# One decode step of cached attention with a ReGLU block: a hand-written program in place of a scheduled one

## The chip, the cores and the metric

The kernel runs on one core of a Trainium2 chip. TensorE (PE) multiplies, VectorE (DVE), ScalarE (ACT) and GpSimd (POOL) work elementwise, SyncE (SP) issues loads; each runs its own instruction queue in order. Sixteen DMA engines carry every load from HBM to the core's memory (SBUF). The metric is the device time of one execution in microseconds.

## The reference

One token `x` (640 values) goes through a layer norm, attention over a cache of 8192 keys and values per head, and a gated block, each with its residual. All data is float32.

```python
H, Dh, Sk, D, F = 32, 192, 8192, 640, 1536
xn = layernorm(x)
q  = (xn @ wq)                               # (H, Dh)
s  = einsum("hd,hkd->hk", q, k_cache) * Dh**-0.5
o  = einsum("hk,hkd->hd", softmax(s), v_cache)
h  = x + o.reshape(H * Dh) @ wo
g  = layernorm(h)
gate = g @ W_gate; gate = gate * (gate > 0)
out = h + (gate * (g @ W_up)) @ W_down
```

K and V are 201 MB each, wq and wo 15.7 MB each, W_up, W_gate and W_down 3.9 MB each: 446 MB that are read once.

## The kernel before

The program is written against a tile framework: pools of buffers hand out tiles, and the framework adds the waits. The order on each engine is the order of the code.

A head's 8192 positions are cut into two tiles of 4096 (`load_kv`, L77). In a tile, partition p holds 32 neighbouring positions, so that each partition's row is one run of 32 x 192 x 4 = 24 KB and a tile is 3 MB. Six buffers of 24 KB rows (pool `kv`) serve K, V, at the start wq and at the end the weights of the gated block.

For a head, `query` (L165) copies the head's q to all partitions through TensorE into PSUM. `scores_of` (L171) multiplies K with q on VectorE, 16 positions an instruction (L178), sums 10 of the 16 on VectorE (L179) and 6 on ScalarE, an instruction each (L181). `softmax_of` (L185) takes the maximum over all partitions through TensorE (L189, L193), then the exponential on ScalarE with its sums (L198) and the total through TensorE (L200). `values_of` (L212) multiplies the weights with V on TensorE, two positions of each partition a matmul, in four groups of rows (L217); `to_columns` (L223) adds the groups through TensorE (L232) and transposes on VectorE (L235).

The loop over heads (L246) issues the loads of K of the next head and V of this one in turn, then the work on V of this head, then scores and softmax of the next. wo is loaded in nine pieces (`load_wo`, L85), each ahead of the first of its four heads (the last two pieces have two heads each), and multiplied behind the last of them (`output_of`, L237). The weights of the gated block are loaded last, in eleven pieces, each as its buffer comes free (L283 to L290). The second layer norm (L295 to L313), the products with W_up and W_gate (L319), the gate (L329) and the product with W_down (L337) follow.

SP issues all of these loads in the order of the code, and a load whose buffer is still in use holds up the loads behind it.

Of the kernel before, what the change touches and what calls it, by code (L numbers as in the profile page):

```python
# [1 line left out]

# [8 lines left out]
AX = mybir.AxisListType  # L11


@with_exitstack
def kernel(
    ctx: ExitStack,
    tc: tile.TileContext,
    x: bass.AP,
    kc: bass.AP,
    vc: bass.AP,  # L20
    wq: bass.AP,
    wo: bass.AP,
    w_gate: bass.AP,
    w_up: bass.AP,
    w_down: bass.AP,
    out: bass.AP,
):
    nc = tc.nc
# [4 lines left out]
    DJ = D // P  # L33
    R = 32
    NCH = S // (P * R)
    NS = S // P
    SUB = 16
    NA = 6
    TW = R * DH
    HPQ = H // NQ  # L40
    QB = 512
    NQB = HPQ * DH // QB
    DG = D // NQ
    FG = F // NQ
    FJ = F // P
    SCALE = DH ** -0.5
    EPS = 1e-5
    GROUPS = [list(range(4 * i, 4 * i + 4)) for i in range(7)] + [[28, 29], [30, 31]]
    group_of = {h: (gi, i) for gi, hs in enumerate(GROUPS) for i, h in enumerate(hs)}
# [3 lines left out]
    const = ctx.enter_context(tc.tile_pool(name="const", bufs=1))  # L53
    kv = ctx.enter_context(tc.tile_pool(name="kv", bufs=6))
    wts = ctx.enter_context(tc.tile_pool(name="wts", bufs=2))
    small = ctx.enter_context(tc.tile_pool(name="small", bufs=2))
    row = ctx.enter_context(tc.tile_pool(name="row", bufs=1))
    ps_q = ctx.enter_context(tc.tile_pool(name="ps_q", bufs=2, space=bass.MemoryType.PSUM))
    ps_x = ctx.enter_context(tc.tile_pool(name="ps_x", bufs=1, space=bass.MemoryType.PSUM))
    ps_o = ctx.enter_context(tc.tile_pool(name="ps_o", bufs=1, space=bass.MemoryType.PSUM))  # L60
    ps_s = ctx.enter_context(tc.tile_pool(name="ps_s", bufs=2, space=bass.MemoryType.PSUM))
    ps_a = ctx.enter_context(tc.tile_pool(name="ps_a", bufs=1, space=bass.MemoryType.PSUM))

    xT = const.tile([P, DJ], F32, name="xT")
    xrow = const.tile([1, D], F32, name="xrow")
    nc.scalar.dma_start(xT, x[0, 0].rearrange("(p j) -> p j", p=P))
    nc.scalar.dma_start(xrow, x[0])


    wq_v = wq.rearrange("(p j) n -> p j n", p=P)  # L70
    wq_ts = []
    for j in range(DJ):
        t = kv.tile([P, TW], F32, name="kv_t")
        nc.sync.dma_start(t, wq_v[:, j, :])
        wq_ts.append(t)

    def load_kv(src, h, c, parts=1):  # L77
        t = kv.tile([P, TW], F32, name="kv_t")
        v = src[h, c * P * R:(c + 1) * P * R, :].rearrange("(p r) d -> p (r d)", p=P)
        n = TW // parts  # L80
        for i in range(parts):
            nc.sync.dma_start(t[:, i * n:(i + 1) * n], v[:, i * n:(i + 1) * n])
        return t

    def load_wo(gi):  # L85
        hs = GROUPS[gi]
        j = len(hs) * DH // P
        t = wts.tile([P, j, D], F32, tag="wo_t", name="wo_t")
        r0 = hs[0] * DH
        nc.sync.dma_start(t, wo[r0:r0 + len(hs) * DH, :].rearrange("(p j) n -> p j n", p=P))  # L90
        return t

    ones = const.tile([P, P], F32, name="ones")
    nc.vector.memset(ones, 1.0)
    eps = const.tile([P, 1], F32, name="eps")
    nc.vector.memset(eps, EPS)
    ident = const.tile([P, P], F32, name="ident")
    from concourse.masks import make_identity
    make_identity(nc, ident)

    sel = const.tile([P, NQ, P], F32, name="sel")
    nc.gpsimd.memset(sel, 0.0)
# [105 lines left out]
    for po in pos:  # L208
        nc.vector.memset(po, 0.0)
# [159 lines left out]
```

## Time and profile before

| | before |
|---|---|
| time, median of 3 runs | 1054.98 us (1054.37 to 1055.05) |
| profiled execution, first to last instruction (span) | 1052.8 us |
| median of the runs over that span | 2.2 us |
| PE, DVE, ACT, POOL busy | 438.6, 727.2, 325.1, 1.9 us |
| bytes moved, mean rate over the span | 446.48 MB, 424 GB/s |
| DMA packets | 22662 |
| mean granted clock of TensorE | 0.668 |

The profiled execution has no time of its own beside its span; the span covers what its instructions show. Busy times are sums over an engine's instructions. The slices that the prediction shows cut the span into 40 equal parts: a DMA digit is the mean busy share of the 16 DMA engines in tenths, and the row below it what they moved. The queue lines give packets, MB and the share of 16 engines' time that the packets took; q1 is SP's queue, q8 and q14 carry instructions, q10 is ScalarE's queue. In a group's row stand line, engine, operation, out<-in, shape, count, then busy us and mean ns of one, then the idle time of the engine ahead of it and what ended it. In the timeline a row is start, us, engine and line, operation and count. Matrix products in float32 leave two records each.

### The profile page before, as it was taken

To read this page: it belongs to the slowest core of one execution; us is meant where nothing else is said; L and a number is where in the kernel's file an instruction comes from. 1 tells how busy PE (TensorE), PEld (TensorE's weight loads), DVE (VectorE), ACT (ScalarE), POOL (GpSimd) and SP (SyncE) were. 2 spreads that over 40 slices of the span, in tenths; PEclk is the share of its full clock that TensorE was granted. 3 is DMA by queue.
4 is the path that set the end of the run, shared out by engine and by line. 5 is a ranking of instruction groups with operands and counts; after the bars stand their busy time and mean duration, and the time that the engine had idled before them with its cause. 6 is when DMAs were issued, how large, how long until landed. Compare 5 with 4: busy or idle time off the path is not lost.

```text
span 1052.8 us, 8858 instructions
## 1 busy us (share of the span) xinstructions
PE 438.6 (42%) x3136; PEld 136.1 (13%) x3136; DVE 727.2 (69%) x418; ACT 325.1 (31%) x1676; POOL 1.9 (0%) x11
## 2 busy tenths in 40 slices
PE   3423444344444333433442444344335334432466
PEld 1101111111111010111110111111101111110122
DVE  1188877677867777687776778677876877777641
ACT  0143333223323332232232333233322322333230
POOL 0000000000000000000000000000000000000000
PEclk9756666666666666766666665766667666666667
DMA  9999999999999999999999999999999999999996
GB/s 394 429 429 431 431 427 430 429 431 431 430 430 427 431 430 428 432 429 429 432 430 430 429 430 430 427 431 430 430 425 433 431 430 430 429 430 429 428 421 247
DMA packets 22662, 446.48 MB, mean 424 GB/s; under 512 B 2645, under 2 KB 2649, under 8 KB 4442
## 3 DMA queue, kind: packets, MB, share of 16 engines
q1 hardware_dynamic: 22472, 445.92, 99.1%
q8 instruction: 24, 0.39, 0.2%
q14 instruction: 20, 0.16, 0.0%
q10 hardware_dynamic: 146, 0.01, 0.0%
HBM read 445.91 MB, written 0.00 MB: 424 GB/s over the span
## 4 chain that ended last, share of the span: by engine, by line
DMA 65%; DVE 25%; PE 8%; ACT 1%; issue 1%; SPq 0%
DMA kv_t<-in_A_k_cache_dram 53%; DVE kv_t L178 18%; DMA kv_t<-in_A_v_cache_dram 8%; DVE sc L179 6%; PE po L217 5%; DMA dn_a<-in_B_W_down_dram 2%; DMA kv_t<-in_A_wq_dram 2%; PE q L168 1%; PE ps_small L232 1%; ACT p L198 0%; PE qp L159 0%; PE ps_small L193 0%; PE ps_small L200 0%; DVE oT L235 0%; PE pd L337 0%
## 5 line engine op out<-in xcount | busy, mean ns | idle before, releaser
L178 DVE TENSOR_TENSOR kv_t<-kv_t,q 128x3072 f32<-128x3072 f32 x128 | 423.4, 3349 | 163.4 <-DMA kv_t<-in_A_k_cache_dram 163.0
L181 ACT ACTIVATE kv_t<-kv_t 128x192 f32<-128x192 f32 x768 | 267.6, 349 | 529.5 <-DVE kv_t L178 529.5
L217 PE MATMUL po<-kv_t,p 128*2 128x384 f32 x2048 | 296.0, 747 | 245.6 <-DMA kv_t<-in_A_v_cache_dram 245.6
L179 DVE TENSOR_REDUCE sc<-kv_t 128x10 f32<-128x1920 f32 x128 | 269.1, 2144 | 0.0
L168 PE MATMUL q<-q,sel 128*128 128x192 f32 x64 | 31.0, 589 | 290.4 <-DVE kv_t L178 290.4
L181 ACT ACTIVATION_READ_ACCUMULATOR kv_t<-kv_t 128x1 f32 x768 | 143.3, 187 | 0.0
L217 PEld LDWEIGHTS po<-kv_t,p 128*2 128x2 f32 x2048 | 60.3, 111 | 449.8 <-DMA kv_t<-in_A_v_cache_dram 271.4
L168 PEld LDWEIGHTS q<-q,sel 128*128 128x128 f32 x64 | 15.7, 303 | 319.4 <-DVE kv_t L178 243.0
L220 ACT ACTIVATE ob<-po,rl 128x384 f32<-128x384 f32 x32 | 18.6, 580 | 113.5 <-PE po L217 113.5
L202 DVE RECIPROCAL rl<-ps_small 128x1 f32<-128x1 f32 x32 | 5.4, 168 | 52.6 <-PE ps_small L200 52.6
L191 DVE TENSOR_REDUCE m<-ps_small 1x1 f32<-1x128 f32 x32 | 8.9, 279 | 42.3 <-PE ps_small L189 42.3
L235 DVE STREAM_TRANSPOSE oT<-ps_small 32x192 f32<-32x192 f32 (+1 forms) x32 | 11.8, 367 | 27.1 <-PE ps_small L232 27.1
L232 PE MATMUL ps_small<-ob,par 128*32 128x192 f32 (+1 forms) x144 | 25.7, 315 | 0.7 <-ACT ob L220 0.7
L159 PE MATMUL qp<-kv_t,xn 128*32 128x512 f32 x120 | 19.4, 801 | 10.1 <-DMA kv_t<-in_A_wq_dram 9.1
L200 PE MATMUL ps_small<-rs,ones 128*128 128x1 f32 x64 | 12.4, 264 | 24.9 <-ACT p L198 24.9
L241 PE MATMUL acc<-wo_t,oT 128*32 128x160 f32 (+1 forms) x408 | 19.9, 352 | 4.6 <-DVE oT L235 4.6
L193 PE MATMUL ps_small<-m,ones 1*128 1x1 f32 x64 | 12.3, 259 | 11.9 <-DVE m L191 11.9
L241 PEld LDWEIGHTS acc<-wo_t,oT 128*32 128x32 f32 (+1 forms) x408 | 14.0, 127 | 9.9 <-DVE oT L235 7.8
L200 PEld LDWEIGHTS ps_small<-rs,ones 128*128 128x128 f32 x64 | 9.7, 191 | 27.6 <-ACT p L198 27.6
L193 PEld LDWEIGHTS ps_small<-m,ones 1*128 1x128 f32 x64 | 9.6, 186 | 18.3 <-DVE m L191 18.3
L232 PEld LDWEIGHTS ps_small<-ob,par 128*32 128x32 f32 x144 | 11.3, 109 | 4.8 <-ACT ob L220 1.4
L198 ACT ACTIVATE p<-sc,nb 128x64 f32<-128x64 f32 x32 | 11.1, 348 | 1.2 <-ACT nb L195 0.2
(77 smaller groups left out, 79.9 us busy)
## 6 DMA issues: line engine op xcount, KB each, us to landing
kv_t<-in_A_k_cache_dram SPq DMA_DIRECT2D x64, 3072.0 KB, 33.7
kv_t<-in_A_v_cache_dram SPq DMA_DIRECT2D x63, 3072.0 KB, 39.7
kv_t<-in_A_wq_dram SPq DMA_DIRECT2D x5, 3072.0 KB, 20.7
wo_t<-in_A_wo_dram SPq DMA_DIRECT2D x7, 1920.0 KB, 43.0
kv_t<-in_A_v_cache_dram SPq DMA_DIRECT2D x4, 768.0 KB, 38.3
up_a<-in_B_W_up_dram SPq DMA_DIRECT2D x1, 3072.0 KB, 33.9
gt_a<-in_B_W_gate_dram SPq DMA_DIRECT2D x2, 1536.0 KB, 24.2
wo_t<-in_A_wo_dram SPq DMA_DIRECT2D x2, 960.0 KB, 41.4
```

Source lines behind the costliest of these rows:

```text
L159: nc.tensor.matmul(qps[b][g * Q:(g + 1) * Q, :], xn[:, j:j + 1].to_broadcast([P, Q]), wq_ts[j][:, c0:c0 + QB], start=(j == 0), stop=(j == ...
L168: nc.tensor.matmul(q[:, 0:DH], sel[:, g, :], q4[:, i * DH:(i + 1) * DH], start=True, stop=True)
L178: nc.vector.tensor_mul(ks, ks, q[:, None, :].to_broadcast([P, SUB, DH]))
L179: nc.vector.reduce_sum(sc[:, i0:i0 + SUB - NA], ks[:, :SUB - NA, :], axis=AX.X)
L181: nc.scalar.activation(ks[:, r, :], ks[:, r, :], AF.Copy, accum_out=sc[:, i0 + r:i0 + r + 1])
L193: nc.tensor.matmul(pb[:, 0:1], ones[0:1, :], m1, start=True, stop=True)
L200: nc.tensor.matmul(pl[:, 0:1], ones, rs, start=True, stop=True)
L217: nc.tensor.matmul(po[g * Q:g * Q + 2, :], p[:, 2 * i:2 * i + 2], vts[c][:, r * DH:(r + 2) * DH], start=(i < NQ), stop=(i >= NP - NQ))
L220: nc.scalar.activation(ob, po, AF.Copy, scale=rl)
L232: nc.tensor.matmul(pt[q0:q0 + Q, 0:W], par[:, k, :], ob[:, k * DH + u * W:k * DH + (u + 1) * W], start=(k == 0), stop=(k == 1))
L235: nc.vector.transpose(oT[s], pt[s, 0:W].rearrange("p (c j) -> p j c", c=Q))
L241: nc.tensor.matmul(acc[g * Q:(g + 1) * Q, :], oT[s, j, :], wo_t[s, j, g * DG:(g + 1) * DG], start=False, stop=(last and j == J - 1))
```

## The change

The program is written by hand, without the framework. A small class, `Eng`, records the operations of one engine; each operation names what it has to wait for, and signals its engine's semaphore or one of its own.

- K and V of a head are one tile each: partition p holds 64 neighbouring positions, a row of 48 KB, 6 MB a load. There are two such buffers for K (`kt`) and one for V (`vt`). wq goes through the same three buffers in three loads.
- q of all heads is spread to all partitions once, at the start (`q_all`); a head's q is copied from there to PSUM by ScalarE (`put_q`), two heads ahead.
- Scores: VectorE multiplies 16 positions an instruction as before; GpSimd adds the upper 96 of the 192 products to the lower 96 (`fold`); VectorE then sums 96 products of all 16 positions. ScalarE has no part in it.
- TensorE's work on a head is the body of a loop that runs 32 times, placed at the first slot of an instruction block: maximum, its spread, the sum of the exponentials, 32 matmuls on V, two matmuls that add the row groups. Its waits count semaphores down.
- A head's output is gathered by VectorE into one row of a tile `oall` (head h in rows 4h to 4h + 3); after the last head it is divided by the sums and brought into columns once.
- wo is loaded behind K and V in three loads (the first behind the last K, before the last V) and multiplied after the last head.
- W_up and W_gate are one load each, W_down five.

Places in the order of the instructions. First TensorE in the steady state. `ident`, `mp`, `m` belong to the maximum, `rs` to the sums, `p` and `pr` are the weights, `ob` the product of a head. Before, this is one head:

```order
L217 MATMUL po_221<-kv_t,p 2x384 x16
L168 MATMUL q<-q_216,sel 128x192
L217 MATMUL po_221<-kv_t,p 2x384 x16
L189 MATMUL ps_small<-ident,mp 1x128
L193 MATMUL ps_small<-m_462,ones 128x1
L200 MATMUL ps_small<-rs,ones 128x1
L232 MATMUL ps_small<-ob,par 32x192 x2
```

After the change this is the loop's body, and it stands once:

```order
L223 MATMUL bank<-ident,mp 1x128 [waits to_pe_mp]
L224 MATMUL bank<-m,ones 128x1 [waits to_pe_m1]
L225 MATMUL bank<-rs,ones 128x1 [waits to_pe_exp]
L231 MATMUL bank<-vt,pr 2x384 [waits dma_v]
L231 MATMUL bank<-vt,pr 2x384 x31
L235 MATMUL bank<-ob,par 128x192 [waits to_pe_ob]
L235 MATMUL bank<-ob,par 128x192
L52 REGISTER_ALU
L52 COMPARE_AND_BRANCH
```

The matmul that copied q is gone from the head, V has one wait in place of two, and the program holds 397 matmuls where it held 1584. ScalarE's program goes from 982 instructions to 195.

VectorE, one head before:

```order
L178 TENSOR_TENSOR kv_t<-kv_t,q 128x3072 [waits DMAHW3_49,DMAHW2_49]
L178 TENSOR_TENSOR kv_t<-kv_t,q 128x3072
L179 TENSOR_REDUCE sc<-kv_t 128x10 [waits DVE_49] x2
L178 TENSOR_TENSOR kv_t<-kv_t,q 128x3072 [waits DMAHW5_49,DMAHW4_49]
L178 TENSOR_TENSOR kv_t<-kv_t,q 128x3072
L179 TENSOR_REDUCE sc<-kv_t 128x10 [waits DVE_49] x2
L187 TENSOR_REDUCE mp<-sc 128x1 [waits DVE_49,Activation_49]
L191 TENSOR_REDUCE m_364<-ps_small 1x1 [waits PE_49]
L202 RECIPROCAL rl<-ps_small 128x1 [waits PE_49]
L235 STREAM_TRANSPOSE oT<-ps_small 32x192 [waits PE_49]
```

and after:

```order
L278 TENSOR_TENSOR kt<-kt,bank 128x3072 [waits s_act,dma_k0]
L278 TENSOR_TENSOR kt<-kt,bank 128x3072 x3
L284 TENSOR_REDUCE sc<-kt 128x16 [waits s_pool] x4
L287 TENSOR_REDUCE mp<-sc 128x1 [waits s_dve]
L290 SCALAR_TENSOR_TENSOR oall<-bank,ind,oall 128x193 [waits s_pe]
L294 TENSOR_REDUCE m<-bank 1x1 [waits s_pe]
```

All four multiplies stand ahead of the reductions, which wait for GpSimd's folds; the gather (L290) of the head before stands between the two maxima and waits for that head's last matmul.

SP at the end, before:

```order
L90 DMA wo_t<-in_A_wo_dram 128x1920
L82 DMA kv_t<-in_A_k_cache_dram 128x6144 [waits DMAHW3_49,DVE_49,Activation_49]
L82 DMA kv_t<-in_A_v_cache_dram 128x6144 [waits DMAHW4_49,PE_49]
L82 DMA kv_t<-in_A_k_cache_dram 128x6144 [waits DMAHW5_49,DVE_49,Activation_49]
L82 DMA kv_t<-in_A_v_cache_dram 128x6144 [waits DMAHW6_49,PE_49]
L82 DMA kv_t<-in_A_v_cache_dram 128x6144 [waits DMAHW7_49,DVE_49,Activation_49]
L82 DMA kv_t<-in_A_v_cache_dram 128x1536 [waits DMAHW0_49,PE_49]
```

and after:

```order
L137 DMA kt<-in_A_k_cache_dram 128x12288 [waits s_dve]
L137 DMA vt<-in_A_v_cache_dram 128x12288 [waits s_pe]
L137 DMA kt<-in_A_wo_dram 128x11520 [waits s_dve]
L137 DMA vt<-in_A_v_cache_dram 128x12288 [waits s_pe]
L137 DMA kt<-in_A_wo_dram 128x11520 [waits s_dve]
L137 DMA vt<-in_A_wo_dram 128x7680 [waits s_pe]
L137 DMA zt<-in_B_W_up_dram 128x7680 [waits s_act]
L137 DMA kt<-in_B_W_gate_dram 128x7680 [waits s_pe]
L137 DMA kt<-in_B_W_down_dram 128x3840 [waits s_pe]
```

wo's pieces among the heads have become three loads at the end, and each load of V waits for TensorE, each load of K for VectorE. SP's queue goes from 157 loads to 78. The core of the diff:

```diff
+class Eng:
+    def op(self, fn, after=(), sig=None, takes=()):
+        ...
+    def emit(self, nc, e):
+        for o in self.ops:
+            if o[0] == "loop":
+                _, n, body = o
+                with nc.Fori(0, n, engines=[self.kind], head_slot={self.kind: 0}):
+                    for fn, waits, takes, sig in body:
+                        self._one(e, fn, waits, takes, sig)
+            else:
+                self._one(e, *o)
+
+    def _one(self, e, fn, waits, takes, sig):
+        for sem, val in takes:
+            e.wait_ge(sem, val).then_inc(sem, -val)
+        ...
-    R = 32
-    NCH = S // (P * R)
     NS = S // P
-    SUB = 16
-    NA = 6
-    TW = R * DH
+    TW = NS * DH
+    SUB = 16
+    NSUB = NS // SUB
+    HD = DH // 2
-    kv = ctx.enter_context(tc.tile_pool(name="kv", bufs=6))
+    kt = [sb(f"kt{i}", P, TW) for i in range(2)]
+    vt = sb("vt", P, TW)
+    zt = sb("zt", P, DJ * F)
...
+    def put_q(h, after):
+        h_qb[h] = act.op(lambda e: e.copy(qb[h % 2][:, 0:DH], q_all[:, h * DH:(h + 1) * DH]), after)
...
+    pe.body, pe.in_body = [], 0
+    pe.op(lambda e: e.transpose(pa[0:1, 0:P], mp, ident), takes=[(to_pe["mp"], 1)], sig=pe.sem)
+    pe.op(lambda e: e.matmul(pb[:, 0:1], ones[0:1, :], m1, start=True, stop=True), takes=[(to_pe["m1"], 1)], sig=pe.sem)
+    pe.op(lambda e: e.matmul(po2[:, DH:DH + 1], ones, rs, start=True, stop=True), takes=[(to_pe["exp"], 1)])
     NP = NS // 2
+    for i in range(NP):
+        g = i % NQ
+        pe.op(lambda e, i=i, g=g: e.matmul(po[g * Q:g * Q + 2, :], pr[:, 2 * i:2 * i + 2],
+                                           vt[:, 2 * i * DH:2 * (i + 1) * DH], start=(i < NQ), stop=(i >= NP - NQ)),
+              takes=[(dma_sems["v"], 16)] if i == 0 else [], sig=pe.sem if i == NP - 1 else None)
+    for k in range(2):
+        pe.op(lambda e, k=k: e.matmul(po2[:, 0:DH], par[:, k, :], ob[:, k * DH:(k + 1) * DH],
+                                      start=(k == 0), stop=(k == 1)),
+              takes=[(to_pe["ob"], 1)] if k == 0 else [], sig=pe.sem if k == 1 else None)
+    body, pe.body = pe.body, None
+    pe.ops.append(("loop", H, body))
...
+    def load_k(h):
+        h_k[h] = load(kt[h % 2], kf[h].rearrange("(p r) d -> p (r d)", p=P), f"k{h % 2}", [h_kfree[h]])
+    def load_v(h):
+        load(vt, vf[h].rearrange("(p r) d -> p (r d)", p=P), "v", [in_loop(h - 1, T_V) if h else h_q[4]])
...
     for h in range(H):
+        if h + 1 < H:
+            load_k(h + 1)
+        else:
+            load_wo(0, h_kfree[H])
+        load_v(h)
+        k3 = kt[h % 2].rearrange("p (r d) -> p r d", d=DH)
+        for i in range(NSUB):
+            ks = k3[:, i * SUB:(i + 1) * SUB, :]
+            a = dve.op(lambda e, ks=ks, h=h: e.tensor_mul(
+                ks, ks, qb[h % 2][:, None, 0:DH].to_broadcast([P, SUB, DH])), [h_k[h], h_qb[h]])
+            fold.append(pool.op(lambda e, ks=ks: e.tensor_add(ks[:, :, 0:HD], ks[:, :, 0:HD], ks[:, :, HD:DH]), [a]))
+        for i in range(NSUB):
+            a = dve.op(lambda e, ks=ks, i=i, h=h: e.reduce_sum(sc[h % 2][:, i * SUB:(i + 1) * SUB], ks[:, :, 0:HD],
+                                                               axis=AX.X), [fold[i]])
+        h_kfree[h + 2] = a
+        dve.op(lambda e, h=h: e.reduce_max(mp, sc[h % 2], axis=AX.X), [a], sig=to_pe["mp"])
+        if h:
+            gather(h - 1)
+        dve.op(lambda e: e.reduce_max(m1, pa[0:1, 0:P], axis=AX.X), [in_loop(h, T_MAX)], sig=to_pe["m1"])
+        a = act.op(lambda e: e.mul(nb, pb[:, 0:1], -SCALE), [in_loop(h, T_ALL)])
+        act.op(lambda e, h=h: e.activation(pr, sc[h % 2], AF.Exp, bias=nb, scale=SCALE, accum_out=rs),
+               [a, h_kfree[h + 2]], sig=to_pe["exp"])
+        if h + 2 < H:
+            put_q(h + 2, [h_mul3[h]])
+        act.op(lambda e: e.copy(ob, po), [in_loop(h, T_V)], sig=to_pe["ob"])
...
+    load_wo(1, h_kfree[H + 1])
+    load_wo(2, in_loop(H - 1, T_V))
+    h_up = load(up_t, rows_of(w_up), "up", [h_qb[H - 1]])
+    h_gt = load(gt_t, rows_of(w_gate), "k0", [h_wof[0]])
+    for n, (j0, j1) in enumerate(((0, 6), (6, 9), (9, 10), (10, 11), (11, 12))):
+        a = load(dn_t[:, j0:j1, :], rows_of(w_down)[:, j0:j1, :], f"dn{n}", [h_wof[1]])
...
-        for i in range(parts):
-            nc.sync.dma_start(t[:, i * n:(i + 1) * n], v[:, i * n:(i + 1) * n])
-                nc.vector.tensor_mul(ks, ks, q[:, None, :].to_broadcast([P, SUB, DH]))
-                nc.vector.reduce_sum(sc[:, i0:i0 + SUB - NA], ks[:, :SUB - NA, :], axis=AX.X)
-                for r in range(SUB - NA, SUB):
-                    nc.scalar.activation(ks[:, r, :], ks[:, r, :], AF.Copy,
-                                         accum_out=sc[:, i0 + r:i0 + r + 1])
```

More of the change, by code (lines that the diff above doesn't have):

```diff
@@ L56 @@
[L56 to L61, printed above, removed]
@@ L93 @@
[L93 to L102, printed above, removed]
-    for g in range(NQ):
-        nc.gpsimd.memset(sel[g * Q:g * Q + 1, g, :], 1.0)
-    par = const.tile([P, 2, Q], F32, name="par")
```

477 lines of the change are left out of this document (236 added, 241 removed).

## The prediction

> **What bounds the kernel now.** I read the page's head, its slices and its queues first, then stretches of the end, then the timeline.
>
> ```profile
> span 1052.8 us, 8858 instructions
> DMA  9999999999999999999999999999999999999996
> GB/s 394 429 429 431 431 427 430 429 431 431 430 430 427 431 430 428 432 429 429 432 430 430 429 430 430 427 431 430 430 425 433 431 430 430 429 430 429 428 421 247
> q1 hardware_dynamic: 22472, 445.92, 99.1%
> q8 instruction: 24, 0.39, 0.2%
> q14 instruction: 20, 0.16, 0.0%
> ```
>
> The DMA queue of SP fills 99.1% of 16 engines' time, and all slices but the last stand at about 430 GB/s. VectorE, the busiest compute engine, has 727 of 1052.8 us. The kernel is bound by moving 446 MB; a compute saving is worth nothing here unless it holds up a load. Every load still issues, 64 K and V pairs included, so what can change is (a) the DMA engines' time per byte, (b) gaps in their work, (c) what follows the last byte. The same view in stretches of the end (us, busy of PE, PEld, DVE, ACT, POOL, clock, DMA share, GB/s):
>
> ```profile
> 500.00:980.00 480.00, 196.00 (x1388) 59.29 (x1388) 353.47 (x189) 156.43 (x819) 0.00 (x0) 0.66 1.00 430
> 1040.00:1043.00 3.00, 1.37 (x32) 0.77 (x24) 1.40 (x2) 0.00 (x0) 0.00 (x0) 0.93 0.62 243
> 1043.00:1045.00 2.00, 1.26 (x20) 0.60 (x16) 0.00 (x0) 0.00 (x0) 0.00 (x0) 0.50 0.28 110
> 1045.00:1047.00 2.00, 1.49 (x24) 0.78 (x20) 0.00 (x0) 0.00 (x0) 0.00 (x0) 0.50 0.06 24
> 1047.00:1049.00 2.00, 2.00 (x40) 1.42 (x34) 0.00 (x0) 0.00 (x0) 0.00 (x0) 0.50 0.05 18
> ```
>
> 430 GB/s over 16 engines is 26.9 GB/s for one. The end tapers: 9 engines' worth at 1040 to 1043, 4 at 1043 to 1045, then for 4 us at most one. All got equal shares of each load, so one engine is some 4 us behind the next ones, and every load's landing waits for it.
>
> **Rows of 48 KB.** Two stretches of the queue, the first almost all 24 KB rows, the second almost all short ones (560 to 620, then 1040 to 1050 us):
>
> ```profile
> q1 hardware_dynamic: 1181, 25.78, 100.3%
> ...
> q1 hardware_dynamic: 331, 1.02, 25.8%
> ```
>
> They are 962.9 us of engine time (100.3% of 16 x 60) and 41.3 us. With a fixed time a per packet and b per MB: 1181a + 25.78b = 962.9 and 331a + 1.02b = 41.3, so a is about 11 ns (9 to 12 with the rounding). Packets of data by the loads' shapes: K and V 131 loads of 128 rows before (V's last tile is in four), 64 after, so 8576 fewer; wq 256, wo 768 and the GLU weights 512 fewer: 10,112. At 11.2 ns over 16 engines that is **-7.1 us**. Ends: 0, if a 48 KB row still goes as two packets or the fixed time doubles with the row; -8.0 with the 79 x 16 completion writes that fall away too (157 loads become 78). I take -7.1, the count times the measured price.
>
> [...]
>
> **Fewer instructions to fetch.** Instruction fetches ride on the same 16 engines: 24 packets of 16 KB, and 16 KB at 26.9 GB/s takes 0.61 us from whichever engine carries it, 14.6 us in all; the 20 of 8 KB take 0.3 us each. PE has 1584 matmuls in the program, 66 to a 16 KB packet; the loop leaves 397, so 6 or 7 packets. ScalarE's 982 program rows become 195, so most of the 20 go as well. If half of the 24 fell on the engine that ends last it loses 7.3 us there, and would lose 2 after. The gain stops where the next engines become last, which the taper puts 4 us earlier: **-4 us**. Ends: 0, if fetches are not why that engine is late; -6, the whole taper (the missing share of the four stretches above sums to 6 us).
>
> **GpSimd folds, ScalarE freed.** Rows of the groups (busy, mean ns of one, idle before):
>
> ```profile
> L178 DVE TENSOR_TENSOR kv_t<-kv_t,q 128x3072 f32<-128x3072 f32 x128 | 423.4, 3349 | 163.4 <-DMA kv_t<-in_A_k_cache_dram 163.0
> L179 DVE TENSOR_REDUCE sc<-kv_t 128x10 f32<-128x1920 f32 x128 | 269.1, 2144 | 0.0
> L102 POOL MEMSET sel<- 128x512 f32 x1 | 0.5, 528 | 0.0
> masks.py:197 POOL MEMSET ident<- 128x128 f32 x1 | 0.2, 204 | 0.3 <-POOLq L355 0.3
> masks.py:199 POOL TENSOR_SCALAR_AFFINE_SELECT ident<-ident 128x128 f32<-128x128 f32 x1 | 0.3, 293 | 0.0
> L220 ACT ACTIVATE ob<-po,rl 128x384 f32<-128x384 f32 x32 | 18.6, 580 | 113.5 <-PE po L217 113.5
> L217 PE MATMUL po<-kv_t,p 128*2 128x384 f32 x2048 | 296.0, 747 | 245.6 <-DMA kv_t<-in_A_v_cache_dram 245.6
> ```
>
> A head's K and V are 12.58 MB, 29.2 us at 430 GB/s: that is the clock each engine must keep. VectorE: 4 multiplies of 3.35 us, 4 reductions of 1536 instead of 1920 elements (2.14 x 0.8 = 1.72 us), about 0.9 us of small ones: 21.2 us. It fits. A fold reads two streams of 1536 and writes one; the trace has none. Below: GpSimd's memset slope, (528 - 204) / 384 = 0.84 ns an element, 1.4 us. Above: twice the select's (293 - 96) / 128 = 1.54 ns for a read and a write, 4.7 us. I take 3.3 us, nearer the top since two reads are nearest to two selects' reads. The last reduction then ends 13.4 + 3.3 + 1.7 or, if VectorE's own queue is longer, 13.4 + 6.9 = 20.3 us after K lands. That term is **0** while VectorE is through its head within 29.2 us: 3.35 + 4F + 1.72 + about 2.2 for the maximum, the gather and the second maximum stays under it for F up to 5.5 us. Past that point each us of F costs 4 us on every head.
>
> **One V buffer, two K buffers, all of 48 KB.** SP's queue is in order, K of the next head, then V, and V waits for the last matmul on the V before it; behind that wait stand the next K and all later loads.
>
> ```profile
> SPq L82 <- DVE sc L179: 830.7, 62, 18.4
> 1015.67 6.82 PE L217 MATMUL po<-kv_t,p 128*2 128x384 f32 x64
> 11.33 0.16 DVE L126 TENSOR_REDUCE s<-xT 128x1 f32<-128x5 f32 x1 [9.46 <-DMA xT<-in_A_x_dram]
> 15.31 6.96 PE L159 MATMUL qp<-kv_t,xn 128*32 128x512 f32 x48 [1.00 <-DVE par L108]
> ```
>
> Let V land at 0. TensorE has waited (its row shows 245.6 us of that), so its 32 matmuls (64 records) take 6.8 us as in this row, or 9.3 by the group (296.0 / 32). The next V is issued at 7 to 9.5. The K in front of it moves until 14.6, so the engines have 5 us of work left when it comes, and the K after it, freed 20.3 us after its landing at -14.6, is issued in the same moment. SP's wait (it waits 830.7 us on scores already) moves, and no gap opens: **0**. VectorE's next head needs the second product of the head before, at 9.3 + ScalarE's 0.6 copy + about 1, then the two maxima: 12.5 at worst against K's landing at 14.6. Margin 2 us, and a late start there would still leave 8 us before K's buffer is missed. The loop's waits and its branch lie in the 16 us that TensorE has free per head. At the start x's 8 small pieces per engine take turns with rows twice as long, so s at 11.33 comes some 7 us later; the first Wq products end near 30 us, and Wq's own bytes (15.7 MB) keep the queue full until 38: **0**.
>
> **The end.** Wo moves behind the last V in three loads, with W_up, W_gate, W_down after. The same bytes; each has its issue well before the queue runs dry (Wo's third needs V's last matmul, 7 to 9.5 us after landing, while Wo's second moves for 13.7). W_gate is one load now and its 20 matmuls start when all has landed, where before 4 were left:
>
> ```profile
> 1037.73 1.50 PE L319 MATMUL pg<-gt_a,hc 128*32 128x384 f32 x16 [2.23 <-DMA gt_a<-in_B_W_gate_dram]
> 1039.59 0.85 PE L319 MATMUL pg<-rest,hc 128*32 128x384 f32 x8 [0.37 <-DMA rest<-in_B_W_gate_dram]
> 1042.08 1.39 PE L337 MATMUL pd<-rest,guT 128*32 128x160 f32 x24 [1.63 <-DVE guT L331]
> 1049.84 0.39 DVE L340 SCALAR_TENSOR_TENSOR o<-pd,hr,h 128x160 f32<-128x160 f32 x1 [7.82 <-PE pd L337]
> 1050.26 0.65 SPq L341 DMA_DIRECT2D out_dram<-o  x1
> ```
>
> Sixteen more at 1.50 / 8 are 3.0 us, so pd begins 5.5 us after W_gate, and 48 of its matmuls at 1.39 / 12 take 5.6 to 6.2: 11.6 us after, where before VectorE's last instruction stood 10.2 us after (1049.84 - 1039.59), paced by the last W_down pieces. **+1.4 us**; 0 to +3.6 (at the cold rate that other rows of L319 show, 4.71 us for 16).
>
> **Sum.** 1052.8 - 7.1 - 4.0 + 1.4 = 1043.1 us of span. The median of the runs, 1054.98, stands 2.2 above this span; so 1045.3, **1045 us**.
>
> **Rivals.** (1) *The loop refetches its body.* If each way back to the top loads a packet again, 32 are added to the 6: 38 against 24 now. With half on the last engine it has 11.6 us instead of 7.3, +4.3; with all on one, 23.2, +15.9. Span 1052.8 - 7.1 + 1.4 + 4.3 to 15.9, time 1054 to 1065, 1058 in the middle: slower. It decides as soon as more than about 10 refetches fall on one engine. For it: the trace has no loop. Against: at 66 matmuls a packet the body's 37 fit in one, and the loop's start is placed at a packet's first slot. [...]
> (2) *GpSimd sets the pace.* A fold over 5.5 us, say 6.0: 4 x 0.5 us on 31 heads, +62, about 1107. The bounds end at 4.7, and the two engines would have to slow each other. The V buffer's chain past 14.6 us is the same kind, a gap at every head.
> (3) *It doesn't do what it says:* rows go as two packets and the last engine stays last. 1052.8 + 1.4 - about 1 for the weights' rows: time 1055, the same.
>
> **How the numbers follow.** Forecast 0.74, (1) 0.09, (2) with its V twin 0.06, (3) 0.11. A measurement here tells about 0.2% from no change. The forecast's ends -8.0, -6, 0 give 1041 below and, with each gain nearly lost, 1052 above; 1040 to 1054 takes in (3) in part and the low end of (1) for 8 in 10. Faster (under 1052.9): the forecast and a quarter of (3), with a little kept back for causes not listed, 0.78. Same: most of (3), 0.09. Slower: (1), (2), 0.13.
>
> **What would show it.** Right: fewer than 12 packets on the instruction queue, some 11,000 on SP's, slices at 432 to 433 GB/s, a taper under 5 us, SP's waits ending on po and not on the scores, multiplies starting as K lands. Wrong: over 30 instruction packets (1); folds over 5.5 us, and multiplies that start behind the second maximum (2); some 20,000 packets or the same taper (3); slices that dip at each head, for V's buffer.

## The result, and the profile after

The changed kernel takes **1042.51 us** (median of 4 runs, 1042.43 to 1043.71), the kernel before on the same chip 1055.01 us: ratio 0.9886, interval 0.9872 to 0.9900, 12.5 us less. 1045 us was forecast, in a range of 1040 to 1054.

The head of the page, the slices and the queues of the changed kernel:

```profile
span 1040.6 us, 7247 instructions
DMA  9999999999999999999999999999999999999997
GB/s 393 443 430 427 437 435 427 438 435 427 436 435 427 436 433 431 433 436 429 433 438 429 433 436 431 431 438 429 429 436 433 431 437 431 431 436 426 438 422 312
q1 hardware_dynamic: 11096, 445.91, 99.4%
q8 instruction: 7, 0.11, 0.0%
q14 instruction: 7, 0.06, 0.0%
```

The bound is the one of before: 16 DMA engines busy 99.4% of the span with the same 446 MB. Half the packets move it, and q8 fell from 24 to 7, q14 from 20 to 7. The middle and the end in stretches:

```profile
500.00:980.00 480.00, 152.09 (x1185) 52.50 (x1177) 330.44 (x178) 21.78 (x83) 218.42 (x64) 0.62 1.00 433
1032.00:1034.00 2.00, 0.36 (x8) 0.16 (x8) 1.40 (x2) 0.00 (x0) 0.00 (x0) 1.00 0.82 320
1034.00:1036.00 2.00, 2.00 (x64) 1.91 (x60) 0.00 (x0) 0.00 (x0) 0.00 (x0) 1.00 0.26 102
1036.00:1038.00 2.00, 1.31 (x40) 0.95 (x32) 0.38 (x1) 0.00 (x0) 0.00 (x0) 1.00 0.04 8
```

433 GB/s where it was 430, and an end in which the share falls from 0.82 to 0.04 in 4 us, where before one engine was still at work 4 us after all others. Each load ends in 16 updates of its semaphore, which I read as one from each DMA engine: the packet records of both traces fall into 16 rows, in each of which a packet starts as the one before it ends, and in a row 8 packets of a K or V load stand between two of 4 bytes. The last load's updates (the time of the first, of the last, and between them), then what follows to the end of the span, read from the trace's semaphore events:

```
          first     last    spread   to the span's end
before   1039.3   1048.9      9.65       3.9
after    1033.3   1036.5      3.24       4.1
```

The fastest engine is done 6.0 us earlier, the slowest 6.4 us nearer to it, and the tail is 0.2 us longer: 12.2 us, the difference of the spans. The groups that carry a head, and SP's longest wait:

```profile
L280 POOL TENSOR_TENSOR kt<-kt 128x1536 f32<-128x1536 f32 x128 | 436.9, 3447 | 522.5 <-DVE kt L278 522.5
L278 DVE TENSOR_TENSOR kt<-kt,bank 128x3072 f32<-128x3072 f32 x128 | 420.7, 3349 | 144.9 <-DMA kt<-in_A_k_cache_dram 144.9
L231 PE MATMUL bank<-vt,pr 128*2 128x384 f32 x2048 | 241.5, 641 | 543.3 <-PEq L60 543.3
L284 DVE TENSOR_REDUCE sc<-kt 128x16 f32<-128x1536 f32 x128 | 215.2, 1744 | 0.0
```

```profile
SPq L137 <- PE bank L231: 887.2, 32, 29.5
```

VectorE's multiplies wait for K's landing, and SP waits for TensorE's V matmuls (the program's `po` shows as `bank`): every engine follows the queue.

### The profile page after: what moved, and what is told of

The parts are those of the page before. It is cut to its first block, busy times and chain, and to the rows that moved or that the text cites. A ratio compares the mean times of both kernels' runs of the same rounds, so it can differ in the third digit from the quotient of the medians.

```text
span 1040.6 us, 7247 instructions
## 1 busy us (share of the span) xinstructions
PE 366.3 (35%) x3056; PEld 134.0 (13%) x3056; DVE 669.0 (64%) x394; ACT 56.1 (5%) x184; POOL 437.6 (42%) x134
## 3 DMA queue, kind: packets, MB, share of 16 engines
q1 hardware_dynamic: 11096, 445.91, 99.4%
## 5 line engine op out<-in xcount | busy, mean ns | idle before, releaser
L280 POOL TENSOR_TENSOR kt<-kt 128x1536 f32<-128x1536 f32 x128 | 436.9, 3447 | 522.5 <-DVE kt L278 522.5
L278 DVE TENSOR_TENSOR kt<-kt,bank 128x3072 f32<-128x3072 f32 x128 | 420.7, 3349 | 144.9 <-DMA kt<-in_A_k_cache_dram 144.9
L231 PE MATMUL bank<-vt,pr 128*2 128x384 f32 x2048 | 241.5, 641 | 543.3 <-PEq L60 543.3
L284 DVE TENSOR_REDUCE sc<-kt 128x16 f32<-128x1536 f32 x128 | 215.2, 1744 | 0.0
L231 PEld LDWEIGHTS bank<-vt,pr 128*2 128x2 f32 x2048 | 58.6, 102 | 706.0 <-issue 706.0
L290 DVE SCALAR_TENSOR_TENSOR oall<-bank,ind,oall 128x193 f32<-128x193 f32 x32 | 13.4, 420 | 142.0 <-PE bank L235 142.0
L301 ACT COPY ob<-bank 128x384 f32<-128x384 f32 x32 | 15.3, 479 | 800.0 <-PE bank L231 800.0
L235 PE MATMUL bank<-ob,par 128*128 128x192 f32 x128 | 28.4, 345 | 22.4 <-PEq L60 22.4
L235 PEld LDWEIGHTS bank<-ob,par 128*128 128x128 f32 x128 | 19.9, 189 | 44.5 <-issue 44.5
L225 PE MATMUL bank<-rs,ones 128*128 128x1 f32 x64 | 14.6, 297 | 27.7 <-PEq L60 27.7
L224 PE MATMUL bank<-m,ones 1*128 1x1 f32 x64 | 11.6, 247 | 21.3 <-PEq L60 21.3
L211 PE MATMUL bank<-zt,ones 1*128 1x512 f32 x24 | 17.3, 1006 | 0.8 <-ACT zt L199 0.8
L297 ACT ACTIVATE pr<-sc,nb 128x64 f32<-128x64 f32 x32 | 11.1, 348 | 1.0
```

Of the source, the lines that this page charges most:

```text
L211: a = pe.op(lambda e, g=g, b=b, o=o: e.matmul(o, ones[g * Q:g * Q + 1, :], q4[g * Q:g * Q + 1, b * QB:(b + 1) * QB], start=True, stop=True ...
L224: pe.op(lambda e: e.matmul(pb[:, 0:1], ones[0:1, :], m1, start=True, stop=True), takes=[(to_pe["m1"], 1)], sig=pe.sem)
L225: pe.op(lambda e: e.matmul(po2[:, DH:DH + 1], ones, rs, start=True, stop=True), takes=[(to_pe["exp"], 1)])
L231: pe.op(lambda e, i=i, g=g: e.matmul(po[g * Q:g * Q + 2, :], pr[:, 2 * i:2 * i + 2], vt[:, 2 * i * DH:2 * (i + 1) * DH], start=(i < NQ), s ...
L235: pe.op(lambda e, k=k: e.matmul(po2[:, 0:DH], par[:, k, :], ob[:, k * DH:(k + 1) * DH], start=(k == 0), stop=(k == 1)), takes=[(to_pe["ob" ...
L278: a = dve.op(lambda e, ks=ks, h=h: e.tensor_mul(ks, ks, qb[h % 2][:, None, 0:DH].to_broadcast([P, SUB, DH])), [h_k[h], h_qb[h]])
```

## The experiments

All times are medians of 2 to 11 runs; "+" is against 1042.51 us. The kernel before was timed beside each group (1054.7 to 1055.0).

### One part undone at a time: loop, rows, both

**The loop written out.**

```diff
-                with nc.Fori(0, n, engines=[self.kind], head_slot={self.kind: 0}):
+                for _ in range(n):
```

> The loop on TensorE is written out 32 times; nothing else differs from the changed kernel. Theory (instruction fetches made one DMA engine late): the instruction queue goes from 7 packets back to about 24, the taper at the end from about 3 us to some 9 us, and the time from 1042.5 to about 1048 (+4 to +7). Rival (the taper came from the number of rows, the loop only shortened the program): 24 packets again, but the same taper and a time within 1 us of 1042.5.

Measured 1045.16 us (ratio to before 0.9909, 0.9894 to 0.9925): **+2.7**. Its instruction queue is that of before:

```profile
q8 instruction: 24, 0.39, 0.2%
```

That is under the forecast of +4 to +7. 17 blocks more cost 0.16 us each, a quarter of the 0.61 us that the prediction put for one on the engine that carries it (their packets last 1.0 to 1.1 us on record). The sixteen landings show why: from 129 us on their spread moves between 2.3 and 4.5 us, it ends at 3.1, and the last engine is never more than 0.8 us behind the second-last. TensorE's blocks do not pile up on one engine. (Shared out evenly, 17 packets of 1.07 us would be an estimated 1.1 us on each engine; why it is 2.7 stays open.)

**Rows of 24 KB**, the same loads as two runs per partition:

```diff
-        load(vt, vf[h].rearrange("(p r) d -> p (r d)", p=P), "v", ...)
+        load(vt.rearrange("p (c n) -> p c n", c=2), vf[h].rearrange("(c p r) d -> p c (r d)", c=2, p=P), "v", ...)
```

and K likewise.

> K and V still come in one load of 6 MB a head, but each partition's row is two runs of 24 KB from two places; the loop stays. Theory (about 11 ns for each packet): 8192 packets more, 5.6 us on every engine, so about 1048 (+4.5 to +6.5), slices at 430 GB/s again and the taper as short as with long rows. Rival (row length costs nothing, the gain was fewer fetches and fewer loads): within 1 us of 1042.5.

Its SP queue, and the stretch 500 to 980:

```profile
q1 hardware_dynamic: 19288, 445.91, 99.4%
```

```profile
500.00:980.00 480.00, 150.79 (x1201) 52.74 (x1193) 330.41 (x178) 21.78 (x83) 218.20 (x64) 0.62 1.00 431
```

1048.43 us (0.9936, 0.9922 to 0.9949): **+5.9**. 8192 packets more on 16 engines make 11.6 ns a packet (5.92 x 16 / 8192); the prediction had worked out 11.2 from two stretches of the trace before. But not all of the 5.9 us is the queue's. In the profiled execution the last load's first update comes 5.2 us later than in the changed kernel's and its last 4.9 us later, which makes 9.6 to 10.2 ns a packet. The rest came after the last landing, from W_gate's matmuls:

```profile
1032.28 6.15 PE L361 MATMUL bank<-kt,hT 128*32 128x384 f32 x40 [4.00 <-DMA kt<-in_B_W_gate_dram]
```

They took 4.88 us in the changed kernel. TensorE's granted clock was 0.50 in the four microseconds from 1032, and 0.93 in the changed kernel's 1030 to 1032. The medians of these short series carry this difference of some 1.3 us, by how many of their runs had the slower end.

**Both.**

> Loop written out and rows of 24 KB together. Theory (the two terms add, and nothing else in the rewrite moved the time): 1042.5 + 5.5 + 5.6, about 1053.5, within 2 us of the kernel before. Rival (something else in the rewrite, folds or Wo's place, gives a share of its own): it stays several us below 1053.

1050.05 us (0.9958, 0.9944 to 0.9971): +7.5, still 4.9 us under before. So the two parts by which the prediction explained its gain do not hold all of it.

### The folds

```diff
-            fold.append(pool.op(lambda e, ks=ks: e.tensor_add(ks[:, :, 0:HD], ks[:, :, 0:HD], ks[:, :, HD:DH]), [a]))
+            fold.append(a)
...
-                ... ks[:, :, 0:HD], axis=AX.X), [fold[i]])
+                ... ks, axis=AX.X), [fold[i]])
```

> GpSimd's folds are taken out; VectorE sums all 192 products itself (four reductions of 3072 elements, about 3.3 us each). Theory (VectorE has room): a head takes it 13.4 + 13.2 + 0.9 = 27.5 us against 29.1 for its K and V, so the time stays at 1042.5 within 1 us, and idle time ahead of the multiplies falls from 145 to below 60 us. Rival (the folds are needed, the chain through the second maximum is too long without them): VectorE sets the pace and the time rises by 10 us or more.

1044.49 us (0.9904, 0.9889 to 0.9919): +2.0, where no more than 1 was forecast. Without folds, ScalarE still idle, VectorE reads each product whole. Its two groups, then a stretch near the start of this kernel, and the same stretch of the changed kernel:

```profile
L278 DVE TENSOR_TENSOR kt<-kt,bank 128x3072 f32<-128x3072 f32 x128 | 420.5, 3345 | 54.1 <-DMA kt<-in_A_k_cache_dram 54.1
L284 DVE TENSOR_REDUCE sc<-kt 128x16 f32<-128x3072 f32 x128 | 419.9, 3340 | 0.0
```

```profile
50.00:100.00 50.00, 22.70 (x90) 7.92 (x89) 43.14 (x16) 7.95 (x16) 0.00 (x0) 0.57 0.98 416
```

```profile
50.00:100.00 50.00, 23.14 (x95) 8.84 (x94) 40.94 (x22) 8.69 (x19) 27.35 (x8) 0.57 1.00 432
```

VectorE at 26.3 us a head for the two groups ((420.5 + 419.9) / 32) still keeps the 29 us clock. What it loses is at the start, where Wq holds the first heads up and K's buffers come back late. GpSimd as such is worth 2 us here; that ScalarE's sums are gone is worth more, as the next runs show.

### Whose instruction blocks make an engine late

In the trace of before the spread of the sixteen landings grows in steps. Spread after a landing (at us: spread), and the 8 KB packets of q14 in the same time, both from the trace's events:

```
before   278:2.6 285:2.9 341:2.9 349:3.6 407:3.6 423:4.2 486:4.3 494:4.9 549:4.9 565:5.6 630:5.6 638:6.3
         694:6.3 709:7.0 768:7.0 776:7.6 839:7.7 854:8.3 913:8.4 916:9.0 976:9.0 992:9.7
q14 at   278 280 345 419 429 486 561 634 702 709 755 772 850 912 988
```

Every 71 us or so a block comes, and at the next landing the last engine is 0.65 to 0.71 us later (the first of these steps, at 285, is 0.3). It falls behind alone: the second-last engine's update is 0.3 us ahead of it at 278 us and 4.1 us ahead at 992. The packets at 278, 429, 709 and 755 have no step of their own. That the blocks take time from the engines that move the data stands in the packet records: as a block's packet ends, a packet of 24 KB begins that takes 1.38 to 1.46 us (22 of q8's 24) or 1.29 to 1.57 us (all of the 15 q14 times above but 912), where the median is 0.914. ScalarE's sums have two instructions each, 1536 in all (L181: 768 ACTIVATE, 768 ACTIVATION_READ_ACCUMULATOR). So: give the changed kernel that many instructions back, with no work in them.

```diff
         act.op(lambda e: e.copy(ob, po), [in_loop(h, T_V)], sig=to_pe["ob"])
+        for i in range(48):
+            a = act.op(lambda e, i=i: e.copy(scr[:, i:i + 1], eps), [h_eps, h_scr], sig=None if i == 47 else False)
+        h_scr = a
```

> The changed kernel with 48 one-element copies more on ScalarE per head, behind its copy of po, where ScalarE has nothing else to do; they compute nothing that is used. 1536 more instructions are 12 more blocks of ScalarE's instruction stream at 128 to a block. Theory A (ScalarE's instruction blocks all ride on one DMA engine and hold it up by about 0.67 us each, and this, not TensorE's blocks, made the last engine late before): that engine gets 12 x 0.67 = 8 us behind, less the 0 to 3 us by which it now may be ahead of the last one: 1047.5 to 1050.5 us, q14 19 packets, and a taper of the last stretch that is longer again. Theory B (ScalarE's blocks spread over the engines, as TensorE's do, or cost nothing): 12 x 0.67 / 16 = +0.5 us, 1043 us, taper as after.

The queue on the page, the group of the copies, and four stretches:

```profile
q14 instruction: 19, 0.16, 0.0%
...
L304 ACT COPY scr<-eps 128x1 f32<-128x1 f32 x1536 | 146.4, 190 | 0.0
```

```profile
500.00:980.00 480.00, 151.71 (x1197) 54.15 (x1189) 330.42 (x178) 96.00 (x899) 218.32 (x64) 0.62 1.00 428
1038.00:1040.00 2.00, 1.11 (x16) 0.21 (x8) 0.70 (x2) 0.00 (x0) 0.00 (x0) 1.00 0.96 383
1040.00:1042.00 2.00, 1.25 (x36) 1.20 (x40) 0.70 (x1) 0.00 (x0) 0.00 (x0) 1.00 0.31 124
1042.00:1044.00 2.00, 2.00 (x68) 1.82 (x56) 0.00 (x0) 0.00 (x0) 0.00 (x0) 1.00 0.05 18
```

1050.40 us (0.9964, 0.9950 to 0.9977): **+7.9**, 0.66 us for each of 12 blocks (q14 from 7 to 19, 128 copies to a block of 8 KB), for copies on an engine that is idle otherwise. Again the last engine steps back by 0.6 to 0.8 us at the landings behind the q14 packets (packets at 303, 363, 448 and 508 us, steps at 304, 377, 451 and 510), with the second-last up to 3.3 us ahead of it. Theory A's time holds; its taper does not: the share falls as fast as after the change, and the loss lies in the rate, 428 GB/s where it was 433. The section on V's buffer says why.

**The sums themselves**, split as before:

```diff
+        NA = 6
...
+            a2 = dve.op(... e.reduce_sum(sc[h % 2][:, i0:i0 + SUB - NA], ks[:, :SUB - NA, :], axis=AX.X), [a])
+            for r in range(SUB - NA, SUB):
+                a3 = act.op(... e.activation(ks[:, r, :], ks[:, r, :], AF.Copy, accum_out=sc[h % 2][:, i0 + r:i0 + r + 1]), [a], ...)
```

> The changed kernel with the split of the row sums of before: VectorE sums 10 of 16 rows whole, ScalarE the other 6 one by one, and GpSimd folds nothing. Loop on TensorE and 48 KB rows stay. Theory A (ScalarE's instruction blocks on one DMA engine): the 768 sums and 768 reads of the accumulator are 12 blocks more on q14; time as with the 48 idle copies, plus up to 2 us for what the run without folds showed: 1047.5 to 1052 us. Theory B (what was left of the gain was in TensorE's loop or in the hand-written order): 1043 to 1044.5 us.

```profile
q14 instruction: 18, 0.15, 0.0%
```

1050.55 us (0.9963, 0.9949 to 0.9977): +8.0, the same as the idle copies. It is the instructions of the sums that cost, not the sums: SP's longest wait is still for TensorE's V matmuls (638.7 us), and K's load, which waits for ScalarE's sums up to 7.2 us, stands behind a V that takes 14.5 us.

**The same count on VectorE**, behind its second maximum:

```diff
+        for i in range(48):
+            a = dve.op(lambda e, i=i: e.tensor_copy(scr[:, i:i + 1], eps), [h_eps, h_scr], sig=None if i == 47 else False)
+        h_scr = a
```

> The changed kernel with 48 one-element copies more per head on VectorE, the same number as the idle copies on ScalarE that cost 8 us, behind its second maximum of each head, where it waits for K anyway (48 short ones are some 3 to 5 us of the 8 it has free). Theory A (what costs is the fetching of instruction blocks by the DMA engines, whichever engine's): VectorE's blocks show as packets on an instruction queue, 12 or so more, and the time goes up by 3 to 8 us, by which DMA engine they ride on. Theory B (it is something that ScalarE's own instructions do): no packets, 1042.5 us within 1.

The same views:

```profile
q14 instruction: 19, 0.16, 0.0%
...
L279 DVE TENSOR_TENSOR kt<-kt,bank 128x3072 f32<-128x3072 f32 x128 | 420.6, 3347 | 67.3 <-DMA kt<-in_A_k_cache_dram 67.3
...
L304 DVE COPY scr<-eps 128x1 f32<-128x1 f32 x1536 | 95.2, 131 | 0.0
```

```profile
500.00:980.00 480.00, 154.74 (x1208) 52.25 (x1200) 380.22 (x948) 20.68 (x79) 219.19 (x65) 0.61 1.00 424
```

1057.65 us (ratio to before 1.0027, 1.0016 to 1.0038): **+15.1**, slower than the kernel before. VectorE still waits for K (67.3 us of idle time in front of its multiplies), and K's buffer is free before V's load goes out (533.8 and 535.6 us in one head), so the copies do not set the pace; the 12 blocks do. Theory A holds in kind (VectorE's blocks show on q14, too) and misses in size: nearly twice as much for as many packets. The first steps of the spread are 1.0 us here (2.4 to 3.4 at 203, 3.4 to 4.4 at 262), 0.67 with ScalarE's. Why a block of VectorE costs more was not settled.

**All three undone at once** (loop, rows, sums; the edits above).

> The changed kernel with three things undone at once: TensorE's loop written out, K and V in rows of 24 KB, and the row sums on VectorE and ScalarE as before, without folds. What is left of the change is the hand-written order, the fewer and larger buffers, Wo behind the last V and the fewer loads. Theory A (these three are the whole of the gain): about the time of before, 1053 to 1057 us. Their effects one by one were +2.7, +5.9 and +8.0 us, 16.6 together, which would be 1059; if that is what comes, the three add up, and the rest of the change costs some 4 us. Theory B (the rest of the change brings something too): 1051 us or less.

```profile
q1 hardware_dynamic: 19288, 445.91, 99.2%
q8 instruction: 24, 0.39, 0.1%
q14 instruction: 18, 0.15, 0.0%
```

1054.47 us, ratio to before 1.0000 (0.9991 to 1.0009): the three parts are the whole of the gain. The hand-written order, the fewer buffers, Wo's place and the fewer loads bring and cost nothing in sum. The same time comes about another way: this run's queue moves 427 GB/s from 500 to 980 us and ends with a spread of 3.4 us, where the kernel before had 430 and 9.65. The parts overlap: singly 2.7, 5.9 and 8.0 us, together 12.0. The sums are worth 8.0 when the rest stays changed and 4.4 when loop and rows are undone as well (1054.47 - 1050.05).

### Does the loop fetch its body again?

The loop's head at another slot, so that the body lies across two blocks, and a body of four heads. (The loop written out fetched 17 blocks more for 31 heads, so one head fills an estimated 0.55 of a block and four fill 2.2. If TensorE's instructions have the 64 bytes that ScalarE's 128 copies to 8 KB give, a block of 16 KB has 256 slots, and a body of an estimated 140 that starts at slot 200 ends in the next.)

```diff
-                with nc.Fori(0, n, engines=[self.kind], head_slot={self.kind: 0}):
+                with nc.Fori(0, n, engines=[self.kind], head_slot={self.kind: 200}):
```

```diff
-                with nc.Fori(0, n, engines=[self.kind], head_slot={self.kind: 0}):
-                    for fn, waits, takes, sig in body:
+                with nc.Fori(0, n // 4, engines=[self.kind], head_slot={self.kind: 0}):
+                    for fn, waits, takes, sig in body * 4:
```

> The changed kernel with the loop's head at slot 200 in place of slot 0 of an instruction block, so that the body lies across two blocks. Rival (1) of the prediction (a way back to the top loads its block again when it has left it): 32 to 64 packets more on q8, 40 or more in all, and if they spread over the engines as the written-out loop's did, 32 x 0.61 / 16 = +1.2 us at least and up to +4: 1044 to 1047 us. Theory (both blocks stay loaded): 7 or 8 packets on q8 and 1042.5 us within 1.

> The changed kernel with a loop of 8 trips whose body holds four heads, some 600 instructions, longer than two instruction blocks. If a block that was left is loaded again on each trip: 8 x 2 or 3 = 16 to 24 packets on q8 beside the others and, as with the loop written out (24 packets, +2.7 us), 1044 to 1045.5 us. If the whole body stays loaded: 8 or 9 packets and 1042.5 us within 1.

The queue with the head at slot 200, then with four heads in the body:

```profile
q8 instruction: 6, 0.10, 0.0%
```

```profile
q8 instruction: 8, 0.13, 0.0%
```

1042.62 us (0.9889, 0.9874 to 0.9904) and 1043.86 us (0.9893, 0.9878 to 0.9909). Nothing is fetched again in either. The second median stands 1.35 us higher, but its last load has landed at 1036.6 us, the changed kernel's at 1036.5; the difference is again W_gate's matmuls, 6.31 us in this profiled execution and 4.88 in the changed kernel's, with a granted clock of 0.50 from 1030 to 1032 and not 0.93:

```profile
1027.35 6.31 PE L361 MATMUL bank<-kt,hT 128*32 128x384 f32 x40 [3.98 <-DMA kt<-in_B_W_gate_dram]
```

The runs of both, as of the changed kernel, fall on two values (1042.5 and 1043.8): of four runs each, one, three and one had the higher. So no cost of either layout is shown. The body of four heads, an estimated 2.2 blocks, was run 8 times and fetched once: 8 packets in the whole program, against 24 with the loop written out. No run has a longer body, so where a loop begins to fetch again is not shown.

### How near V's single buffer is to a gap

```diff
-        load(vt, ..., "v", [in_loop(h - 1, T_V) if h else h_q[4]])
+        load(vt, ..., "v", [in_loop(h, T_ALL) if h else h_q[4]])
```

> The changed kernel with V's load waiting for TensorE's second small product of the next head, not for the last matmul on the V before: it is issued some 2.7 us later after V's landing (10 in place of 7.3 us), and so are all loads behind it. By the prediction's working (the K in front of it moves until 14.6 us) the engine that ends last still has work in hand: 1042.5 us within 1.5. If the margin was smaller than I think, each us too late costs 31 heads: +20 us and more.

SP's wait, now for the second small product, then the DMA view from 560 to 620 us (a digit for each 1.5 us), and the same view of the changed kernel:

```profile
SPq L137 <- PE bank L224: 887.3, 31, 30.0
```

```profile
DMA  9999799997799999699999699995997999989999
DMA packets 576, 25.17 MB, mean 419 GB/s; under 512 B 64, under 2 KB 64, under 8 KB 64
```

```profile
DMA  9998999999999997999999999989999999999989
DMA packets 592, 25.95 MB, mean 433 GB/s; under 512 B 64, under 2 KB 64, under 8 KB 64
```

1064.91 us (1.0091, 1.0075 to 1.0106): **+22.4** for an issue that comes 9.5 to 11.1 us after V's landing (13.3 at the first head) and not 6.8 to 8.5, 2.7 us later on average; the queue shows holes, and the forecast of no change failed. The landings say what the margin is made of. V has landed when the last engine's part has; the load of the next V is issued 6.8 to 8.5 us after that, 7.8 on average. By then the fastest engine, which is ahead by the spread, has that much less of K in front of it (K lands 14.5 us after V). Spread at the landings:

```
changed      never over 3.4
copies, sums grows in steps to between 4.4 and 5.0, is cut back, grows again, from 420 us on
VectorE's    5.2 at 321 us, then between 3.3 and 5.6
V later      2.7 until 100 us, 1.0 at 116, then between 0.9 and 3.2
before       grows to 9.7 without a stop
```

With one V buffer the spread has a ceiling near 5 us. An estimate from the traces gives 4.1 to 5.8: 14.5 less 7.8 less the time from issue to an engine's first packet, which in the run after this one is 0.95 us for the first of 16 packets and up to 2.6 us for the last. Past the ceiling the engines that are ahead run dry before the next V's packets come, and what they could have carried is lost. The changed kernel stays 1.5 us under it. Issued 2.7 us later, the ceiling is 1.4 to 3.1 by the same sum, the spread that the changed kernel has (2.5 to 3.4) no longer fits under it, and the heads pay 0.7 us each on average. They do not pay evenly: beside the changed kernel's landings, 1.9 us are lost by 116 us, nothing more until 247 us, while the spread is 0.9 to 1.1, and the rest from 263 us on, when it has grown again. This is also why ScalarE's copies show as a lower rate and not as a taper: the blocks push one engine back to the ceiling, and from there all wait for it. That the spread is cut there is read from landings; that the issue's time sets the price is what this run and the next one show.

```diff
-        load(vt, ..., "v", [in_loop(h - 1, T_V) if h else h_q[4]])
+        load(vt, ..., "v", [in_loop(h - 1, T_V) if h else h_q[4], h_k[h + 1] if h + 1 < H else None])
```

> The changed kernel with V's load waiting also until the next head's K, which stands before it in the queue, has landed: the queue runs empty once per head. This is the prediction's rival (2) in its V form, made to happen. From issue to first bytes and to the landing's semaphore some 2 to 3 us each head, and the fastest DMA engines wait some 3 us more for the last one: 31 x 2 to 3 = 62 to 93 us, 1105 to 1135 us, and slices that dip at each head. If the time hardly moves, the engines' queues hold more than I think.

SP's wait, and stretches around one gap:

```profile
SPq L62 <- DMA kt<-in_A_k_cache_dram: 964.1, 31, 31.6
```

```profile
516.00:518.00 2.00, 0.51 (x4) 0.48 (x4) 0.52 (x2) 0.83 (x4) 0.00 (x0) 1.00 1.08 467
518.00:520.00 2.00, 0.20 (x2) 0.11 (x1) 0.00 (x0) 0.00 (x0) 0.00 (x0) 0.63 0.23 98
520.00:522.00 2.00, 0.00 (x0) 0.00 (x0) 1.31 (x1) 0.00 (x0) 0.00 (x0) 0.50 1.00 295
522.00:524.00 2.00, 0.00 (x0) 0.00 (x0) 2.00 (x2) 0.00 (x0) 0.00 (x0) 0.50 0.28 98
```

1140.90 us (1.0816, 1.0796 to 1.0836): +98.4, 3.2 us for each of 31 gaps. (Bytes count when their packet of 1.8 us ends, so one gap shows as two dips.) The forecast was 62 to 93, from an estimated 2 to 3 us a head; from issue to an engine's first packet this run shows 0.95 to 2.6 us.

## Why the prediction was right, and where it was not

**Rows of 48 KB, -7.1.** The mechanism holds, and the price nearly: 11.6 ns a packet by the medians, 9.6 to 10.2 by the landings, against 11.2. The K and V rows alone are worth 5.9 us by the medians of the run with 24 KB rows, 4.9 to 5.2 at the queue. The other 1920 of the 10,112 packets, most of them the weights', were not tried alone.

**Fewer instructions to fetch, -4.** This is the step that failed. It took as its case that "half of the 24 fell on the engine that ends last", that is TensorE's blocks, at 0.61 us each, and priced ScalarE's by their bytes, 0.3 us. TensorE's blocks do not pile up: the whole loop is worth 2.7 us. ScalarE's smaller blocks did: ten steps of 0.65 to 0.71 us and one of 0.3 on the last engine, from 285 us to 992 us. Taking its sums away is worth 8.0 us, or 4.4 where loop and rows stay as before. Both together were put at 4 and are some 6 to 7: 12.0 for all three less 4.9 to 5.9 for the rows. The trace of before had shown it: the times of the q14 packets stood beside the landings, and the prediction read only packet sizes and counts.

**Folds and ScalarE freed, 0.** A fold takes 3.447 us, forecast 3.3 within 1.4 to 4.7; VectorE's multiply beside it is unchanged at 3349 ns. No term of the time, as said. But the step named it as work moved off ScalarE and saw no gain in that; of the three parts, each undone alone, it was the largest.

**One V buffer, 0.** The value is right, the margin was too wide. The V matmuls lie in the forecast 6.8 to 9.3 us, 7.14 and 7.95 in these two heads:

```profile
521.45 7.14 PE L231 MATMUL bank<-vt,pr 128*2 128x384 f32 x64 [17.15 <-PEq L60]
528.66 0.33 SPq L137 DMA_DIRECT2D vt<-in_A_v_cache_dram  x1
550.53 7.95 PE L231 MATMUL bank<-vt,pr 128*2 128x384 f32 x64 [17.84 <-PEq L60]
```

The "5 us of work left" was meant as room to spare. It is the ceiling for the spread, and 3.4 us of it are in use.

**The start, 0.** x's sum comes 7.8 us later (forecast some 7), and the queue stays full over it (393 and 443 GB/s in the first two slices, 394 and 429 before). x's small packets in one of the 16 rows stand 0.914 us apart before and 1.82 us after, as long as one packet of 24 KB and one of 48 KB:

```profile
19.13 0.16 DVE L172 TENSOR_REDUCE s<-xT 128x1 f32<-128x5 f32 x1 [17.92 <-DMA xT<-in_A_x_dram]
```

**The end, +1.4.** The last rows of the timeline:

```profile
1027.32 4.88 PE L361 MATMUL bank<-kt,hT 128*32 128x384 f32 x40 [3.10 <-DMA kt<-in_B_W_gate_dram]
1033.84 3.47 PE L375 MATMUL bank<-kt,guT 128*32 128x160 f32 x96 [1.64 <-DVE guT L372]
1037.46 0.38 DVE L379 SCALAR_TENSOR_TENSOR o<-bank,hr,h 128x160 f32<-128x160 f32 x1 [3.67 <-PE bank L375]
```

From the first W_gate matmul to VectorE's last instruction it is 10.1 us, forecast 11.6: the W_down matmuls began 6.5 us after W_gate and not 5.5, but ran back to back in 3.5 us, not 5.6 to 6.2. From the last landing the tail is 0.2 us longer, so the term was 0.2 and not 1.4 in this execution. In an execution with the slower end, as the profiled one with four heads in the body, the same tail is 5.5 us, 1.6 longer than before; one of the changed kernel's four runs had the time of it.

**Sum.** Forecast -7.1 - 4.0 + 1.4 = -9.7, measured -12.2 in the spans. That the time was right within 2.5 us is in part luck: two parts of the gain were smaller than thought (rows by 1.2 to 2.2 at most, the loop), and a part that had been priced too low was larger.

**The rivals.** (1) is out in all three layouts tried: no block of the loop came twice. (2) did not come, but its V form stood near: V's issue 2.7 us later would have made the change slower than before. (3) is out by q1's 11,096 packets.

## What to carry to other kernels

Where the DMA queue is the bound, count each engine's instructions too: 1536 one-element copies on an engine with time to spare cost 8 or 15 us here, because their 12 instruction blocks (q14 from 7 packets to 19) are fetched by the engines that move the data. Put the packet times of the instruction queues beside the spread of a load's sixteen landings before you say which engine's program makes the last one late. A single buffer's margin runs from the last engine's landing to the first engine's running dry, so subtract the spread, and test the margin by issuing a little later (2.7 us later cost 22.4 us here). When medians differ by a microsecond, compare the landings of the last load first: here up to 1.3 us of it came after them, from TensorE's clock.

## What the runs showed of the hardware that was not expected

- ScalarE's and VectorE's blocks of 8 KB both appear on q14 and cost far more than their bytes: 12 of them cost 7.9 us (ScalarE) and 15.1 us (VectorE), where 17 of TensorE's 16 KB cost 2.7 us. Why they differ stays open, and so does which DMA engine carries them, since the records do not name it.
- GpSimd adds two streams of 1536 elements in 3.447 us, with VectorE's multiply unchanged beside it (3349 ns with it, 3345 ns in the run without folds).
- The same 20 W_gate matmuls (40 records) took 4.88 us in one execution and 6.15 and 6.31 in two others, whose granted clock stood at 0.50 for longer; that moves the end of this kernel by some 1.3 us.
- A loop body of an estimated 2.2 instruction blocks, run 8 times, is fetched once (8 packets on q8 in the whole program).
